# Expert stage of a Fourier filter and mixture of experts: low parts of the splits moved from GpSimd to VectorE, and both weight matrices laid out on the host in the order of the products

## The chip, the core and the metric

The kernel runs on one core of a Trainium2 chip. The metric is the device time in microseconds (us) of one execution; the median of three runs is given, and one more execution was profiled. The engines are named as in the profile: PE is TensorE (PEld its weight loads), DVE is VectorE, ACT is ScalarE, POOL is GpSimd, SP is SyncE. All inputs lie in device memory when the time starts, so what the host does to lay out an input is no part of the metric.

## The reference

Cut to what matters. First a filter along the sequence in the frequency domain, then a capacity-limited top-1 assignment of tokens to experts, then two products with a ReLU between them.

```python
x: (8, 2496, 256); filt_r, filt_i: (1249, 256); w_gate: (256, 8); w1: (8, 256, 1024); w2: (8, 1024, 256)
X = np.fft.rfft(x, axis=1)
y = np.fft.irfft(X * (filt_r + 1j * filt_i)[None], n=2496, axis=1)
x = y.reshape(19968, 256)
logits = x @ w_gate
# all (token, expert) pairs in falling order of logit; a token goes to the first expert
# that still has room, and each expert takes cap = 19968 // 8 = 2496 tokens
for e in range(8):
    mask = assigned == e
    h = np.maximum(x[mask] @ w1[e], 0.0)
    out[mask] = h @ w2[e]
```

## The kernel before

The first part, up to some 448 us of the profiled execution, is the filter: transforms as products on PE, the filter on DVE and POOL, the inverse transforms, and the filtered tokens written to a DRAM array `xs`. Nothing of it is touched by the change. `x` and the filter are already laid out on the host for it (`lay_x`, `lay_filter`).

The second part, the expert stage, handles the eight experts one after the other. An expert's 2496 tokens are taken in five groups of up to 512 (`g` = 0 to 4; the last has 448). For a group, POOL gathers the tokens' rows by indirect DMA into `xg` (line 784). PE transposes them (`ptr`, line 798, in `turn`). Then comes the first product, `pz` (line 820, eight blocks `f` of 128 hidden units), and the second, `py` (line 869). ACT copies `py` to `y`, and POOL writes `y` to the tokens' places by indirect DMA (line 880).

Every product is made in a reduced float32 form of three terms, high by high, high by low, and low by high. So each operand is split: a rounded copy, the high part, by ACT, and the difference from it, the low part, by another engine.

- Tokens: `xo` is the high part (ACT, line 801), `z` the low part (DVE, line 802).
- Hidden units: `hl` holds both. ACT writes the high half (line 826). The low half is written by DVE straight from PSUM (line 834; line 837 for the last group). For some blocks (odd `f` below 7, groups 1 to 3, while the routing of the next expert is in its search) ACT makes a second, unrounded copy `hr` (line 829) and POOL subtracts (line 830), since POOL can't read PSUM. There are 29 of these.
- Weights: `w0h`, `w0l` are the parts of the first matrix, `w1h`, `w1l` those of the second. An indirect DMA brings each matrix into `wr` (line 763, 128 partitions of 8 KB). `split` then handles eight pieces of 128x512 for an expert: high part on ACT (line 777), low part on POOL, except the first four pieces of the first expert, which are on DVE (line 778). A partition of `wr` holds two rows of `w1` as they lie in DRAM, and hidden units are taken eight apart. So the pieces of the first matrix are read with a step of eight elements and written densely. The columns of `xg` are taken two apart to match (line 796).

While PE works on one expert, the routing of the next runs beside it, most of it on DVE, with small products on PE (`rt`) in between. Its search has eleven rounds per expert (`counts`, `threshold`): `Gm` on DVE, a product, `t`, `D`, `X` on DVE, a product, then `mx`, `o`, `di`, `thr` on DVE. Then the assignment is updated (`M`, `tmp`, `ar`, `asg`, `val`, `r`, ...), and `places` makes the indices of the tokens in five steps: `oa` and `OH` on DVE, a product, `loc` on DVE, two sums on ACT (`junka`), `ex`, `js`, `xid`, `t1b`, `oid` on DVE. The eight weight pieces of the next expert are split in the same stretch of time.

PE's order in this stage is written out by hand: generators yield after a piece of work, and `Pump.feed` puts the next step of the routing between two pieces when a hand-set lag has passed. The order on ACT, DVE and POOL is made by the framework's scheduler. Each engine works through its own queue in order. `tc.issue_after` holds an instruction back to a point of the program.

Of the kernel before, what the change touches and what calls it, by code (L numbers as in the profile page):

```python
# [7 lines left out]
F32, F32R = mybir.dt.float32, mybir.dt.float32r  # L8
# [4 lines left out]
B, N, D, E8, FF = 8, 2496, 256, 8, 1024  # L13
# [96 lines left out]
def lay_filter(re, im):  # L110

    k, j = np.arange(K1)[:, None], np.arange(J)[None]
    fr = np.where(j < 32, k + 39 * j, 39 * (j - 31) - k)
    f = np.stack([np.asarray(re)[fr], np.asarray(im)[fr]])
    return np.ascontiguousarray(f.reshape(2, K1, J, 2, 128).transpose(4, 3, 1, 0, 2)).reshape(128, -1)


class Fft:
# [626 lines left out]
class Ffn:  # L745


    def __init__(s, tc, i, xs, out, cp, ww, zp, ps):
        s.tc, s.nc, s.xs, s.out, s.ww, s.zp, s.ps = tc, tc.nc, xs, out, ww, zp, ps
        s.w1 = i['moe_w1'].rearrange("e (q k) f -> (e q) (k f)", k=2)  # L750
        s.w2 = i['moe_w2'].rearrange("e (q f) d -> (e q) (f d)", f=8)
        s.id = cp.tile([128, 128], F32, name="id")
        make_identity(s.nc, s.id)
        s.scat = []
        s.wt, s.xg, s.xT = {}, {}, {}
# [9 lines left out]
    def split(s, e, part):  # L765

        nc = s.nc
        raw, hl = s.wt[e]
        k, h = divmod(part, 4)
        src, (hi, lo) = raw[k], hl[k]  # L770
        if k == 0:
            h, j = divmod(h, 2)
            src = src.rearrange("p (j q f) -> p j f q", j=2, f=8)[:, j, 4*h:4*h+4]
            hi, lo = (t.rearrange("p (j f q) -> p j f q", j=2, f=8)[:, j, 4*h:4*h+4] for t in (hi, lo))
        else:
            src, hi, lo = (t[:, 512*h:512*h+512] for t in (src, hi, lo))
        nc.scalar.copy(hi, src)
        (nc.gpsimd if e or part >= 4 else nc.vector).tensor_tensor(lo, src, hi.bitcast(F32), op=OP.subtract)

    def gather(s, e, g, ids):  # L780
        for t in range(4*g, 4*g + 4):
# [5 lines left out]
    def turn(s, e, g, h):  # L787

        nc = s.nc
        if h == 0:  # L790
            s.xT[e, g] = [s.zp.tile([128, 2, 512], F32R, name=t, tag=t, bufs=n) for t, n in (('xo', 2), ('z', 3))]
        p = s.ps.tile([128, 2, 256], F32, name="ptr", tag="c", bufs=4)
        w = 0
        for t in range(2):
            n = min(128, CAP - 128*(4*g+2*h+t))
            x = s.xg[e, 4*g+2*h+t].rearrange("p (q k) -> p k q", k=2)
            for k in range(2):
                nc.tensor.transpose(p[:, k, 128*t:128*t+n], x[:n, k], s.id[:n, :n])  # L798
            w += n
        hi, lo = (t[:, :, 256*h:256*h+w] for t in s.xT[e, g])  # L800
        nc.scalar.copy(hi, p[:, :, :w])
        return nc.vector.tensor_tensor(lo, p[:, :, :w], hi.bitcast(F32), op=OP.subtract).ins  # L802

    def run(s, e, pump, hook):
# [7 lines left out]
        def first(g, f):  # L812
            n = min(512, CAP - 512*g)
            xh, xl = s.xT[e, g]
            p = s.ps.tile([128, 512], F32, name="pz", tag="c", bufs=4)
            m = 0
            for k in range(2):
                sl = slice(1024*k+128*f, 1024*k+128*f+128)
                for w, x in ((w1h, xh), (w1h, xl), (w1l, xh)):
                    nc.tensor.matmul(p[:, :n], w[:, sl], x[:, k, :n], start=m == 0, stop=m == 5)  # L820
                    m += 1
                yield 0.65 * n / 512
            hl = s.wp.tile([128, 1024], F32R, name="hl", bufs=NH)
            hs.setdefault(g, []).append(hl)
            h, l = (hl[:, 512*k:512*k+512] for k in range(2))
            s.lasta = nc.scalar.activation(h[:, :n], p[:, :n], AF.Relu).ins  # L826
            if f % 2 == 1 and f < 7 and 0 < g < 4 and s.busy():
                r = s.wp.tile([128, 512], F32, name="hr", bufs=2)
                nc.scalar.activation(r[:, :n], p[:, :n], AF.Relu)
                nc.gpsimd.tensor_tensor(l[:, :n], r[:, :n], h[:, :n].bitcast(F32), op=OP.subtract)  # L830
            else:

                if g < 4:
                    nc.vector.scalar_tensor_tensor(l[:, :n], p[:, :n], 0.0, h[:, :n].bitcast(F32), op0=OP.max, op1=OP.subtract)  # L834
                else:
                    for a, b, c in ((384, n, n), (0, 384, 512)):
                        nc.vector.scalar_tensor_tensor(hl[:, c:c+b-a], p[:, a:b], 0.0, h[:, a:b].bitcast(F32), op0=OP.max, op1=OP.subtract)  # L837

        def firsts(g, count):
            for f in range(len(hs.get(g, ())), min(8, len(hs.get(g, ())) + count)):  # L840
# [50 lines left out]
def emit(tc, i, out):  # L891
    nc = tc.nc
    with ExitStack() as st:
# [31 lines left out]
        def after():  # L925
            nonlocal W
            q = 5
            for k in range(len(rest)):
                if k == 3 + NZ + MZ:
                    fst.close()  # L930
                    R.wb = pool(st, "rb", reuse_waits="tile")
                    W = Ffn(tc, i, xs, out, R.cp, pool(st, "ffw", reuse_waits="tile"), f.zp, ps)
                    W.busy = lambda: pump.kind in 'GX' and not split
                    f.zo = pool(zst, "zo", reuse_waits="tile")
                for c in f.inv2_parts(*rest[k], f.cps):
                    if q < 10:
# [140 lines left out]
                s.step_main()  # L1077


_INS = ['moe_w_gate', 'moe_w1', 'moe_w2']  # L1080


# [13 lines left out]
```

## Time and profile before

| | us |
|---|---|
| median of 3 runs | 1513.62 (1508.94 to 1519.25) |
| the profiled execution | 1514.13 |
| its span in the trace | 1512.4 |
| PE, PEld, DVE, ACT, POOL busy in it | 1411.4, 1234.2, 938.3, 714.0, 628.0 |

The span runs from the first instruction to the last, and 1.7 us of the profiled execution lie around it. A busy engine is one with an instruction under way; matmuls overlap, so PE can be busy and yet not at its peak. "Idle before" a group is the time in which its engine had nothing under way just ahead of it, and what is named behind the arrow ended that wait.

### The profile page before, as it was taken

How to read it: one execution, taken by the hardware profiler on the slowest of the kernel's cores; microseconds unless marked ns; L12 is line 12 of the kernel's file. 1: busy time of each engine (PE TensorE's matmuls, PEld its weight loads, DVE VectorE, ACT ScalarE, POOL GpSimd, SP SyncE). 2: the span in 40 equal slices, each digit the busy share in tenths (PEclk: the TensorE clock that was granted, in tenths of full speed). 3: DMA queues.
4: the chain of work that ended last, by engine and by line, in shares of the span. 5: the costliest groups of instructions: out<-in, count | busy, mean ns of one | idle time of the engine just before them, and what ended most of it. 6: DMA issues, size and time to landing. Idle time of an engine off the chain costs nothing.

```text
span 1512.4 us, 27201 instructions
## 1 busy us (share of the span) xinstructions
PE 1411.4 (93%) x10310; PEld 1234.2 (82%) x10310; DVE 938.3 (62%) x2500; ACT 714.0 (47%) x1705; POOL 628.0 (42%) x619
## 2 busy tenths in 40 slices
PE   4999999988977998999999899899899899999998
PEld 4998999965536887888798888798788789889998
DVE  3666676744567778667857977966866853532321
ACT  3666667634565345436424534533542544532332
POOL 0343344421006426544644654634635544433312
PEclk9999999998997999999999999899999999999999
DMA  9655663578992102102212112111211321111100
GB/s 267 187 150 132 168 179 71 138 214 252 339 349 88 44 31 86 58 20 91 62 34 77 46 52 82 46 44 38 91 32 52 115 72 48 38 49 41 44 25 27
DMA packets 56249, 150.61 MB, mean 100 GB/s; under 512 B 10824, under 2 KB 31432, under 8 KB 51921
## 3 DMA queue, kind: packets, MB, share of 16 engines
q0 software_dynamic: 17840, 60.34, 12.3%
q10 hardware_dynamic: 29407, 46.10, 10.1%
q1 hardware_dynamic: 8872, 42.44, 9.9%
q8 instruction: 81, 1.33, 0.4%
q14 instruction: 49, 0.40, 0.1%
HBM read 85.17 MB, written 63.70 MB: 98 GB/s over the span
## 4 chain that ended last, share of the span: by engine, by line
PE 64%; DVE 15%; ACT 7%; issue 7%; DMA 4%; ACTq 2%; POOL 1%; POOLq 0%; DVEq 0%; SPq 0%
PE py L869 22%; PE pz L820 21%; PE p L191 4%; PE pv L365 4%; PE p L204 3%; PE pa L259 2%; ACT Y L197 2%; PE ptr L798 2%; PE rt L528 2%; ACTq L273 2%; PE pa L223 2%; DVE hl L834 1%; ACT lg L688 1%; DMA xs<-xo 1%; DVE OH L719 1%
## 5 line engine op out<-in xcount | busy, mean ns | idle before, releaser
L869 PE MATMUL py<-w1h,hl 128*128 128x256 f32 x2496 | 490.0, 289 | 7.2 <-DVE hl L837 6.0
L869 PEld LDWEIGHTS py<-w1h,hl 128*128 128x128 f32 x2496 | 406.5, 193 | 11.1 <-DVE hl L837 7.4
L869 PE MATMUL py<-w1l,hl 128*128 128x256 f32 (+1 forms) x1280 | 361.8, 285 | 0.0
L880 POOL DMA_INDIRECT out<-y,oid x160 | 174.6, 1091 | 378.1 <-ACT y L879 335.8
L826 ACT ACTIVATE hl<-pz 128x512 fp32r<-128x512 f32 (+1 forms) x320 | 187.0, 587 | 227.9 <-PE pz L820 206.0
L820 PE MATMUL pz<-xo,w0h 128*128 128x512 f32 (+1 forms) x640 | 267.3, 418 | 15.2 <-DVE hl L834 5.5
L820 PE MATMUL pz<-z,w0h 128*128 128x512 f32 (+1 forms) x640 | 250.3, 391 | 0.8 <-DVE z L802 0.8
L820 PE MATMUL pz<-xo,w0l 128*128 128x512 f32 (+1 forms) x640 | 250.7, 392 | 0.0
L869 PEld LDWEIGHTS py<-w1l,hl 128*128 128x128 f32 (+1 forms) x1280 | 244.1, 191 | 1.9
L834 DVE SCALAR_TENSOR_TENSOR hl<-pz,hl 128x512 fp32r<-128x512 f32 x227 | 155.2, 687 | 130.1 <-ACT hl L826 129.5
L784 POOL DMA_INDIRECT xg<-xs,xid x160 | 168.7, 1055 | 98.1 <-PE ptr L798 33.6
L879 ACT COPY y<-py 128x256 f32<-128x256 f32 x152 | 56.2, 371 | 284.6 <-PE py L869 255.0
L820 PEld LDWEIGHTS pz<-xo,w0h 128*128 128x128 f32 x640 | 123.7, 193 | 36.1 <-DVE hl L834 7.7
L197 ACT COPY Y<-p 64x240 f32<-64x240 f32 (+1 forms) x304 | 116.0, 382 | 60.2 <-PE p L191 15.2
L820 PEld LDWEIGHTS pz<-xo,w0l 128*128 128x128 f32 x640 | 122.1, 191 | 24.5
L820 PEld LDWEIGHTS pz<-z,w0h 128*128 128x128 f32 x640 | 123.2, 192 | 17.0 <-DVE z L802 1.6
L191 PE MATMUL p<-cS,xr 117*128 117x120 f32 x688 | 102.9, 298 | 27.9 <-ACT Y L197 18.7
L212 POOL TENSOR_TENSOR P<-P 128x256 f32<-128x256 f32 x80 | 58.5, 731 | 167.5 <-DVE P L210 166.4
L191 PEld LDWEIGHTS p<-cS,xr 117*128 117x128 f32 x688 | 93.7, 212 | 32.2 <-ACT Y L197 21.6
L520 DVE TENSOR_TENSOR Gm<-M,thr 117x1232 bf16<-117x1232 f32 (+2 forms) x80 | 105.9, 1334 | 0.2
L729 ACT ACTIVATE junka<-rt,loc 128x176 bf16<-128x176 f32 x160 | 65.5, 410 | 70.5 <-DVE loc L726 43.9
L204 PE MATMUL p<-cW,Y 128*128 128x128 f32 x640 | 89.1, 278 | 0.6 <-ACT Y L197 0.6
(219 smaller groups left out, 2254.5 us busy)
## 6 DMA issues: line engine op xcount, KB each, us to landing
zd<-zt ACTq DMA_DIRECT2D x160, 128.0 KB
z<-zd SPq DMA_DIRECT2D x26, 600.0 KB
xs<-xo ACTq DMA_DIRECT2D x22, 600.0 KB
xr<-x SPq DMA_DIRECT2D x7, 1344.0 KB
xr<-x SPq DMA_DIRECT2D x7, 1064.0 KB
xs<-Y ACTq DMA_DIRECT2D x10, 600.0 KB
F<-filt ACTq DMA_DIRECT2D x2, 1280.0 KB
xg<-xs,xid POOLq DMA_INDIRECT x160, 2.8
```

The costliest lines, as they stand in the source:

```text
L191: s.lastmm = nc.tensor.matmul(p[:, q-q0, :120], xv[:, q-24*h], s.cS1, start=True, stop=True).ins
L197: (nc.vector.tensor_copy if t in ((5,) if b else (1, 3, 5, 7, 9)) else nc.scalar.copy)(dst, src)
L204: nc.tensor.matmul(p[:, k], s.Y1[b][:, 4*g+k, dh*128:dh*128+128], s.cW[:, 4*g+k], start=True, stop=True)
L365: nc.tensor.matmul(p[:120, :w], s.cD, z[:, g-g0:g-g0+w], start=True, stop=True)
L520: nc.vector.tensor_tensor(Gm[:, s0:s1, :m], s.M[:, s0:s1].unsqueeze(2).to_broadcast([117, s1 - s0, m]), thr[:117].unsqueeze(1).to_broadcas ...
L729: nc.scalar.activation(s.junka, pr[:, h, :S], AF.Sign, bias=loc[:, c:c+1], scale=-1.0, accum_out=js[:, c:c+1])
L784: s.lastg = s.nc.gpsimd.indirect_dma_start(out=xg[:n], out_offset=None, in_=s.xs, in_offset=bass.IndirectOffsetOnAxis(ap=ids[0][:n, t:t+1] ...
L820: nc.tensor.matmul(p[:, :n], w[:, sl], x[:, k, :n], start=m == 0, stop=m == 5)
L826: s.lasta = nc.scalar.activation(h[:, :n], p[:, :n], AF.Relu).ins
L834: nc.vector.scalar_tensor_tensor(l[:, :n], p[:, :n], 0.0, h[:, :n].bitcast(F32), op0=OP.max, op1=OP.subtract)
L869: nc.tensor.matmul(p[:a.stop-a.start], hs[g][f][:, a], b[:, 256*f:256*f+256], start=m == 0, stop=m == 8 * len(terms) - 1, skip_group_check ...
L880: st = nc.gpsimd.indirect_dma_start(out=out_rows, out_offset=bass.IndirectOffsetOnAxis(ap=ids[1][:w, 4*g+t:4*g+t+1], axis=0), in_=y[:w], i ...
```

## The change

Four edits, all for the expert stage.

1. The host lays out both weight matrices (`lay_w1`, `lay_w2`), so that partition q of `wr` holds rows q and 128+q of `w1`, and rows q, 128+q, ... of `w2`. The 8 KB of a partition are one run in DRAM, as before.
2. `split` reads and writes every piece densely. The pieces come in the same order as before.
3. The low part of every weight piece, and of every `hl`, is made on DVE. The second ACT copy `hr` goes.
4. `turn` takes the columns of `xg` as two halves instead of every other one.

```diff
+def lay_w1(w):
+    return np.ascontiguousarray(np.asarray(w).reshape(E8, 2, 128, FF).transpose(0, 2, 1, 3)).reshape(E8 * 128, 2 * FF)
+def lay_w2(w):
+    return np.ascontiguousarray(np.asarray(w).reshape(E8, 8, 128, D).transpose(0, 2, 1, 3)).reshape(E8 * 128, 8 * D)
...
-        s.w1 = i['moe_w1'].rearrange("e (q k) f -> (e q) (k f)", k=2)
-        s.w2 = i['moe_w2'].rearrange("e (q f) d -> (e q) (f d)", f=8)
+        s.w1, s.w2 = i['w1'], i['w2']
...
-        src, (hi, lo) = raw[k], hl[k]
-        if k == 0:
-            h, j = divmod(h, 2)
-            src = src.rearrange("p (j q f) -> p j f q", j=2, f=8)[:, j, 4*h:4*h+4]
-            hi, lo = (t.rearrange("p (j f q) -> p j f q", j=2, f=8)[:, j, 4*h:4*h+4] for t in (hi, lo))
-        else:
-            src, hi, lo = (t[:, 512*h:512*h+512] for t in (src, hi, lo))
+        o = 512 * (h if k else 2 * (h % 2) + h // 2)
+        src, hi, lo = (t[:, o:o+512] for t in (raw[k], *hl[k]))
         nc.scalar.copy(hi, src)
-        (nc.gpsimd if e or part >= 4 else nc.vector).tensor_tensor(lo, src, hi.bitcast(F32), op=OP.subtract)
+        nc.vector.tensor_tensor(lo, src, hi.bitcast(F32), op=OP.subtract)
...
-            x = s.xg[e, 4*g+2*h+t].rearrange("p (q k) -> p k q", k=2)
+            x = s.xg[e, 4*g+2*h+t].rearrange("p (k q) -> p k q", k=2)
...
-            if f % 2 == 1 and f < 7 and 0 < g < 4 and s.busy():
-                r = s.wp.tile([128, 512], F32, name="hr", bufs=2)
-                nc.scalar.activation(r[:, :n], p[:, :n], AF.Relu)
-                nc.gpsimd.tensor_tensor(l[:, :n], r[:, :n], h[:, :n].bitcast(F32), op=OP.subtract)
+            if g < 4:
+                nc.vector.scalar_tensor_tensor(l[:, :n], p[:, :n], 0.0, h[:, :n].bitcast(F32), op0=OP.max, op1=OP.subtract)
             else:
...
-                    W.busy = lambda: pump.kind in 'GX' and not split
```

The order of PE's and SP's instructions stays the same, row for row. Those of POOL, ACT and DVE move.

On POOL, a place in the handover from the first expert to the second, before (`wr` is the loaded weights, `xg` a gather, `out` a write of results):

```order
L784 DMA xg<-xs,xid 128x256 x4
L880 DMA out<-y,oid 19968x256
L778 TENSOR_TENSOR w0l<-wr_6668,w0h 128x512
L778 TENSOR_TENSOR w1l<-wr_6669,w1h 128x512 x2
L784 DMA xg<-xs,xid 128x256 x4
L880 DMA out<-y,oid 19968x256
L778 TENSOR_TENSOR w1l<-wr_6669,w1h 128x512
L880 DMA out<-y,oid 19968x256
```

and the same place now:

```order
L788 DMA xg<-xs,xid 128x256 x4
L878 DMA out<-y,oid 19968x256 x2
L788 DMA xg<-xs,xid 128x256 x4
L878 DMA out<-y,oid 19968x256 x2
L788 DMA xg<-xs,xid 128x256 x4
```

The subtractions between gathers and writes are gone; only indirect DMAs are left on POOL from here to the end.

On DVE, the same handover, before (`hl` 64 and 384 wide is the last group's low part, for which `py` waits; `OH` belongs to the places):

```order
L837 SCALAR_TENSOR_TENSOR hl<-pz,hl 128x64
L837 SCALAR_TENSOR_TENSOR hl<-pz,hl 128x384
L726 TENSOR_TENSOR loc<-sidx,rt 128x2
L730 TENSOR_SCALAR ex<-rt 128x4
L719 SCALAR_TENSOR_TENSOR OH<-iota,BC,oa 117x512
L837 SCALAR_TENSOR_TENSOR hl<-pz,hl 128x64
L837 SCALAR_TENSOR_TENSOR hl<-pz,hl 128x384
L694 TENSOR_TENSOR asg<-asg,u_6796 117x176
```

and now:

```order
L835 SCALAR_TENSOR_TENSOR hl<-pz,hl 128x64
L835 SCALAR_TENSOR_TENSOR hl<-pz,hl 128x384
L736 TENSOR_TENSOR loc<-sidx,rt 128x2
L729 SCALAR_TENSOR_TENSOR OH<-iota,BC,oa 117x512
L835 SCALAR_TENSOR_TENSOR hl<-pz,hl 128x64
L835 SCALAR_TENSOR_TENSOR hl<-pz,hl 128x384
L782 TENSOR_TENSOR w1l<-wr_6655,w1h 128x512
L740 TENSOR_SCALAR ex<-rt 128x4
```

A weight piece now stands between the `hl` pairs, and `ex` has moved behind it. The other seven pieces of this expert are spread over the same handover in the same way.

On DVE in the search for the second expert, before:

```order
L537 TENSOR_REDUCE D_5875<-t_5874 112x7
L538 TENSOR_TENSOR X_0_3654<-D_5875,row 112x49
L565 TENSOR_REDUCE mx_5807<-rt 128x7
L578 SCALAR_TENSOR_TENSOR o_5894<-mx_5807,pw 128x7
L580 TENSOR_REDUCE di<-o_5894 128x1
```

and now:

```order
L547 TENSOR_REDUCE D_5871<-t_5870 112x7
L548 TENSOR_TENSOR X_0_3654<-D_5871,row 112x49
L832 SCALAR_TENSOR_TENSOR hl<-pz,hl 128x512
L575 TENSOR_REDUCE mx_5805<-rt 128x7
L588 SCALAR_TENSOR_TENSOR o_5888<-mx_5805,pw 128x7
L590 TENSOR_REDUCE di<-o_5888 128x1
```

A low part that POOL made before now stands between `X` and `mx`, where DVE has handed a product to PE and needs its result next.

## Rows read from the trace of the kernel before

**Rows 1.** Page, busy time of PE over the span

```profile
PE 1411.4 (93%) x10310; PEld 1234.2 (82%) x10310; DVE 938.3 (62%) x2500; ACT 714.0 (47%) x1705; POOL 628.0 (42%) x619
```

**Rows 2.** Windows: stretch, length, busy PE, PEld, DVE, ACT, POOL, then PEclk, DMA

```profile
528.00:548.00 20.00, 20.00 (x160) 17.59 (x158) 14.65 (x37) 6.17 (x12) 4.52 (x4) 1.00 0.06 21
...
588.00:608.00 20.00, 15.84 (x111) 14.38 (x110) 15.27 (x48) 6.96 (x24) 12.02 (x11) 0.83 0.13 41
...
708.00:728.00 20.00, 17.55 (x115) 15.76 (x114) 20.00 (x53) 12.81 (x35) 17.61 (x14) 1.00 0.19 58
...
948.00:968.00 20.00, 16.68 (x103) 14.35 (x102) 18.92 (x44) 10.61 (x29) 16.97 (x12) 0.90 0.17 54
...
1208.00:1228.00 20.00, 19.20 (x118) 16.71 (x119) 12.52 (x46) 9.15 (x28) 11.25 (x11) 0.87 0.36 118
```

**Rows 3.** Waits of PE from 448 to 1512: total us, times, longest

```profile
PE rt L725 <- DVE ex L730: 7.7, 5, 4.6
...
PE py L869 <- DVE hl L837: 6.0, 5, 2.3
...
PE rt L528 <- DVE ex L730: 0.3, 1, 0.3
```

**Rows 4.** Timeline: DVE, POOL and PE around 588, PE at two other stalls

```profile
585.30 5.08 DVE L719 SCALAR_TENSOR_TENSOR OH<-iota,BC,oa 117x512 f16<-117x512 f16 x1
...
585.71 1.66 POOL L778 TENSOR_TENSOR w0l<-wr,w0h 128x512 fp32r<-128x512 f32 x1
587.33 2.50 POOL L778 TENSOR_TENSOR w1l<-wr,w1h 128x512 fp32r<-128x512 f32 x2
...
591.04 0.50 PE L869 MATMUL py<-w1h,hl 128*128 128x256 f32 x2 [2.33 <-DVE hl L837]
...
498.23 0.57 PE L528 MATMUL rt<-A,Gm 117*128 117x112 bf16 x8 [1.41 <-DVE Gm L520]
...
1291.86 0.38 PE L869 MATMUL py<-w1h,hl 128*128 128x256 f32 x1 [1.11 <-DVE hl L834]
```

**Rows 5.** One line of DVE: ns min/median/max, then its group with the mean

```profile
L733 DVE TENSOR_SCALAR js<-js x40: 151/160/3199, 442.2 to 1317.1; 128x4 f32<-128x4 f32 x40
...
L733 DVE TENSOR_SCALAR js<-js 128x4 f32<-128x4 f32 x40 | 18.3, 458 | 0.0
```

**Rows 6.** Lines: ns min/median/max, first and last start; the last row a group

```profile
L777 ACT CAST w0h<-wr x32: 1109/1204/1298, 456.8 to 1287.0; 128x512 fp32r<-128x512 f32 x32
L777 ACT CAST w1h<-wr x32: 610/622/648, 463.7 to 1289.7; 128x512 fp32r<-128x512 f32 x32
...
L778 DVE TENSOR_TENSOR w0l<-wr,w0h x4: 1077/1082/1092, 458.0 to 461.1; 128x512 fp32r<-128x512 f32 x4
...
L648 DVE TENSOR_TENSOR asg<-asg,ga x7: 328/334/336, 428.7 to 1173.3; 117x176 f32<-117x176 f32 x7
...
L609 DVE TENSOR_TENSOR tmp<-tmp,val x6: 1608/1612/3399, 468.9 to 1088.5; 117x1408 f32<-117x1408 f32 x6
...
L834 DVE SCALAR_TENSOR_TENSOR hl<-pz,hl 128x512 fp32r<-128x512 f32 x227 | 155.2, 687 | 130.1 <-ACT hl L826 129.5
```

**Rows 7.** Waits in the whole span: total us, times, longest

```profile
DVE t L536 <- PE rt L528: 70.8, 54, 2.6
...
DVE mx L565 <- PE rt L541: 46.3, 53, 2.6
...
POOL w0l L778 <- ACT w0h L777: 31.6, 10, 7.7
```

**Rows 8.** Timeline of the first expert's start: ACT, DVE, POOL, PE

```profile
456.82 4.21 ACT L777 CAST w0h<-wr 128x512 fp32r<-128x512 f32 x4 [8.93 <-DMA wr<-moe_w,widx]
...
457.99 4.16 DVE L778 TENSOR_TENSOR w0l<-wr,w0h 128x512 fp32r<-128x512 f32 x4 [10.75 <-ACT w0h L777]
...
458.87 0.98 POOL L784 DMA_INDIRECT xg<-xs,xid  x1 [0.30 <-issue]
...
462.05 0.80 PE L820 MATMUL pz<-xo,w0h 128*128 128x512 f32 x1 [2.14 <-ACT xo L801]
```

More of the change, by code (lines that the diff above doesn't have):

```diff
@@ L826, in first @@
             s.lasta = nc.scalar.activation(h[:, :n], p[:, :n], AF.Relu).ins
-            if f % 2 == 1 and f < 7 and 0 < g < 4 and s.busy():
-                r = s.wp.tile([128, 512], F32, name="hr", bufs=2)
-                nc.scalar.activation(r[:, :n], p[:, :n], AF.Relu)
-                nc.gpsimd.tensor_tensor(l[:, :n], r[:, :n], h[:, :n].bitcast(F32), op=OP.subtract)
-            else:
[L833 to L837, printed above, removed]
+            if g < 4:
+                nc.vector.scalar_tensor_tensor(l[:, :n], p[:, :n], 0.0, h[:, :n].bitcast(F32), op0=OP.max, op1=OP.subtract)
+            else:
+                for a, b, c in ((384, n, n), (0, 384, 512)):
+                    nc.vector.scalar_tensor_tensor(hl[:, c:c+b-a], p[:, a:b], 0.0, h[:, a:b].bitcast(F32), op0=OP.max, op1=OP.subtract)
         def firsts(g, count):
@@ L1077, in until @@
                 s.step_main()
-_INS = ['moe_w_gate', 'moe_w1', 'moe_w2']
+_INS = ['moe_w_gate']
 def kernel(**inputs):
@@ L1088 @@
     arrays.update(x=lay_x(inputs['x']), filt=lay_filter(inputs['filt_r'], inputs['filt_i']))
+    arrays.update(w1=lay_w1(inputs['moe_w1']), w2=lay_w2(inputs['moe_w2']))
     arrays.update(constants())
```

## The prediction

> **What bounds the kernel now.** I read the page's busy shares first: PE is busy 93% of the span [rows 1]. PE's order does not change, so the time can only move by PE's waits and by its clock. Next came the windows of 20 us. In a search stretch (528 to 548) PE is busy all 20.00 us with DVE at 14.65. Where one expert hands over to the next, PE loses time and DVE is nearly full: PE has 15.84 in 588 to 608, 17.55 in 708 to 728 with DVE at 20.00, 16.68 in 948 to 968 with DVE at 18.92 [rows 2]. From 1228 on, with almost no routing left, PE is nearly always full.
>
> The waits of PE say who is late. Between 448 and 1512 thirteen groups of waits end on DVE, the largest 7.7 us and the smallest 0.3, 40 us in all [rows 3]. The rest is 11 us for the first gather and 2 us for ACT. None of them ends on POOL.
>
> But POOL makes DVE late. The timeline at 585 shows it: `OH` starts on DVE at 585.30 and takes 5.08 us. POOL subtracts three weight pieces from 585.71 to 589.83, and `OH` ends half a microsecond later; then `hl` comes, then PE, which had waited 2.33 us [rows 4]. `js`, on four numbers a partition, has a median of 160 ns, a maximum of 3199 and a mean of 458: (458 - 160) x 40 = 11.9 us on one line [rows 5]. I summed the time above the usual for every DVE instruction from 440 us on. Of those more than 0.15 us over it, 57 overlap a POOL subtraction (`OH` at 585 is the longest), and they lose 72 us: some 60 next to weight pieces, 11 next to `hl`, the rest next to both a subtraction and an indirect DMA. Instructions of DVE that read PSUM, such as `hl`, are not among them. So DVE pays for the work that POOL was given to spare it.
>
> **The change, part by part.**
>
> Weight pieces on DVE: 60 move there (64 less the four that were there). No row shows a dense 128x512 subtraction of two SBUF operands. Two rows on either side bound it: `asg` with 176 columns at 334 ns and `tmp` with 1408 at 1612 [rows 6] lie on a line of 1.04 ns a column, which gives 0.68 us at 512. The stepped pieces on DVE, 1.08 us [rows 6], are the upper end. I take 0.68, since the step is gone. New work: 60 x 0.68 = 40.8 us; the four old ones fall by 4 x 0.40 = 1.6.
>
> Low parts of `hl` on DVE: 29 x 0.687 = 19.9 us [rows 6], all in the search.
>
> Taken from DVE: the 72 us. So DVE has 40.8 - 1.6 + 19.9 - 72 = -13 us net. It matters where: in the handovers +39 against -60, in the search +20 against -12.
>
> Handovers. For each stall of PE I followed DVE's unbroken run of work back from what ended it, summed the lost time in the run, and counted in the new order what now stands in the same run. At 585 to 595 PE stalls 1.68 + 2.33 + 0.31 + 1.52 = 5.84 us (the 2.33 in [rows 4]); the run holds 6.87 us of lost time and gets three pieces, 3 x 0.68 = 2.04. Net -4.8, so most of the stall goes. Nine such places, from 498 (1.41 us) to 1292 (1.11 us) [rows 4], hold 27.5 us of stalls, 36.0 of lost time and 15.0 of new work. Taking at each place the smaller of its stall and its net gain, 18 us go. The new order also moves routing work behind the awaited instruction (`tmp` at 966, the `js` group at 1209), worth some 5 us, and small stalls next to POOL give one more: -24 us. The ends are -15 (the net gain 36 - 15 = 21, less a quarter for new waits) and -31 (all of PE's stalls that stand next to POOL's arithmetic). Stalls with no lost time in front, at 695, 938 and 1182, 5.2 us together, stay.
>
> The clock. PE's granted clock falls to 1.2 GHz for some microseconds after a stall: 0.83 in 588 to 608, 0.90 in 948 to 968, 0.87 in 1208 to 1228 [rows 2]. Seven windows of this kind between them lose 20 x (1 - clock), together 17 us, of which PE was idle part of the time; some 15 us are real. The stalls at 938 and 1182 had no such fall, so not every stall costs it. If three quarters of the stalls go I take -9, with the ends -3 and -15.
>
> Start. ACT's four high parts of `w0` take 4.21 us in the first expert [rows 8]; dense they take the 622 ns of `w1h` instead of 1204 [rows 6], so 2.5. The token copies `xo` behind them, and so the first `pz` at 462.05 [rows 8], come forward by 1.7 at most; the second pair of transposes limits it to 1.5. Behind that the four `w1` pieces, 2.7 us, now stand on DVE ahead of `tmp`, where POOL's delays of 2.9 us fall away: nothing. Sum -1.5 (0 to -2.5).
>
> Here a rule speaks against the change. Next to four stepped subtractions of two SBUF operands on DVE, POOL issues indirect DMAs with gaps of 0.30 us [rows 8], and the four take 1077 to 1092 ns each [rows 6]: none waited for a DMA. The Trainium skill (SBUF — State Buffer, "SBUF: two separate sides") has a DVE instruction with two SBUF inputs and a GpSimd instruction that reads SBUF lock each other out of a shared port for the whole instruction. By that rule POOL's subtractions explain the 72 us, but the indirect DMAs, which read their indices from SBUF, would go on to hold up the new pieces; the sum would lose some 10 us of the gain on DVE (a rival, below). The trace agrees with the first half and not with the second.
>
> Search. The 19.9 us of `hl` go where DVE waits for PE: 70.8 us for `t` and 46.3 us for `mx` [rows 7]. The new order puts them there, ahead of `mx`, or behind `di`. Cover: these 117 us; without it each costs up to 0.69, 20 us in all. The other end is the 12 us of lost time in the same rounds. PE is full there now, so little can be won; I take +3 (+10 to -3).
>
> Nothing: ACT's 29 copies `hr` and its shorter `w0h` (ACT is busy 47% [rows 1]); POOL's gathers and writes, which come earlier but are not waited for after the first; the transposes, whose groups of four follow each other no slower than the dense ones of the filter; the weight loads, 128 runs of 8 KB as before.
>
> Sum, against the profiled execution: 1514.1 - 24 - 9 - 1.5 + 3 = 1482.6; that execution stands 0.5 above the median. **Forecast 1483 us.**
>
> **The rivals.**
>
> Everything goes: all stalls next to POOL and all falls of the clock, and the search costs nothing: 1514.1 - 31 - 15 - 2.5 = 1465. For it: lost time exceeds new work at nearly every stall. Against: pieces still stand in the chains on which PE waits, and a stall of 1 us suffices for some.
>
> A swap: DVE's queue is as full as before and only what fills it changes. If stalls shrink in proportion to DVE's net relief, 13 of 72, then 31 us give 5.6, and with the start 1.5: 1507. For it: DVE at 20.00 of 20 in 708 to 728, and six pieces in that run. Against: the count in the runs.
>
> DVE waits for ACT, and the kernel is slower. POOL now spends 31.6 us waiting for ACT's high parts of `w0` [rows 7]. On POOL nobody minds; on DVE a piece at the head of the queue holds up `hl`, for which PE waits. If DVE took all of it in the handovers: 41 + 32 against 60 lost, 13 us more on DVE than before, straight on PE where it stalls already, and some 6 more for clock: 1514 + 19 = 1533. It decides from the point where these waits exceed 60 - 39 = 21 us. Against it: in the new order most pieces stand behind instructions that, in the old trace, ran after ACT was done; by that comparison the others wait some 13 us, and ACT is faster now.
>
> The lock also holds against indirect DMAs. POOL is busy 42% of the span [rows 1], a third without the arithmetic that goes; 60 pieces, a third of them meeting an indirect DMA of some 0.98 us [rows 8] half done, make 10 us on DVE, half of it on PE: 1488, and 1490 with the clock. The rule is that of the Trainium skill cited above; [rows 6, 8] speak against it.
>
> That the change doesn't do what it says: PE's order is the same, all 89 subtractions stand on DVE and none on POOL, so I give it nothing.
>
> **How the numbers follow.** Forecast 0.57 (own range 1468 to 1499), everything goes 0.15, lock 0.03, swap 0.18, slower 0.07. The range leaves out the slower case, the lower half of "everything goes" and the ends of the swap: 1463 to 1508. A difference of 1% (15 us) is about what a measurement of this kernel can tell from none; the three runs spread over 0.7%. Faster by over 1%, below 1498.5: the forecast almost whole, everything, lock: 0.74. Within 1%: the swap and the forecast's upper end: 0.19. Slower: 0.07.
>
> **What the profile after would show.** `OH`, `js`, `tmp`, `t` on DVE with maxima near their medians; if the maxima stay, the step from POOL to DVE is wrong. Dense pieces at 0.68 us on DVE and 0.62 on ACT. DVE's busy time some 13 us lower. PE's waits on DVE at 15 us or so, and at least four of the seven falls of the clock gone. PE still full in the search; if `rt` there waits for `X` or `Gm`, the `hl` pieces cost more than I took. Waits of DVE's `w0l` and `w1l` for ACT over 20 us would mean the slower rival. The forecast is wrong if PE's stalls come from the length of the chain DVE, PE, ACT in `places` itself and not from DVE's lost time.

## The result and the profile after

The kernel after takes 1462.64 us (median of four runs, 1457.65 to 1466.76) where the kernel before took 1515.01 beside it: a ratio of 0.9657 with a 95% interval of 0.9628 to 0.9685. That is 52 us faster. The forecast was 1483, with a range from 1463 to 1508; the median lies 0.4 us under its low end.

The profiled execution of after took 1464.14 us with a span of 1461.9, 50.5 us less than the span before. The page's busy times and its row of PE's clock come first; they answer to [rows 1].

```profile
PE 1387.9 (95%) x10310; PEld 1214.2 (83%) x10310; DVE 912.8 (62%) x2589; ACT 682.9 (47%) x1676; POOL 493.2 (34%) x530
...
PEclk9999999998997999999999999999999999999999
```

PE does the same 10310 instructions in 23.5 us less busy time; some 16 us of that is time that it no longer spends at 1.2 GHz (table below). DVE has 89 instructions more and 25.5 us less busy time. The clock row has no digit below 9 after the thirteenth slice, where the experts begin. The row of before has one 8 there:

```profile
PEclk9999999998997999999999999899999999999999
```

The windows of 20 us, with the columns of [rows 2]. The work comes 4 us earlier than before in the first of them and 40 to 47 in the last, so one window does not hold the same instructions in both traces.

```profile
528.00:548.00 20.00, 20.00 (x158) 18.19 (x157) 15.25 (x38) 4.73 (x10) 2.96 (x3) 1.00 0.06 21
588.00:608.00 20.00, 19.46 (x135) 15.84 (x134) 17.42 (x63) 12.22 (x37) 15.65 (x15) 1.00 0.31 92
708.00:728.00 20.00, 19.01 (x152) 16.91 (x151) 15.78 (x62) 10.64 (x36) 12.58 (x12) 1.00 0.25 80
948.00:968.00 20.00, 19.03 (x155) 17.38 (x154) 14.19 (x71) 8.57 (x26) 6.59 (x6) 1.00 0.13 42
1208.00:1228.00 20.00, 20.00 (x138) 19.03 (x137) 6.61 (x17) 6.94 (x14) 7.59 (x8) 1.00 0.13 43
```

588 to 608 is the clearest: PE is busy 19.46 us of 20 instead of 15.84, at a clock of 1.00 instead of 0.83.

What PE waited for from 440 us on (answers to [rows 3]; total us, times, longest):

```profile
PE ptr L802 <- DMA xg<-xs,xid: 11.1, 1, 11.1
PE pz L824 <- DVE hl L832: 4.8, 3, 1.9
PE rt L538 <- DVE t1b L749: 2.3, 1, 2.3
...
PE rt L735 <- DVE ex L740: 0.9, 1, 0.9
```

The first gather still costs its 11 us. The waits on DVE add up to some 14 us where they were 40, and the largest of them in [rows 3], on `ex`, has gone from 7.7 to 0.9.

The DVE instructions that POOL used to stretch, and the weight pieces (ns min/median/max; answers to [rows 4 to 6]; the lines of the routing stand ten further down than before, those of the experts' block four, and two further up behind ACT's high part of `hl`):

```profile
L729 DVE SCALAR_TENSOR_TENSOR OH<-iota,BC,oa x40: 729/744/753, 434.5 to 1250.5; 117x512 f16<-117x512 f16 x40
...
L743 DVE TENSOR_SCALAR js<-js x40: 147/158/315, 442.8 to 1267.4; 128x4 f32<-128x4 f32 x40
...
L619 DVE TENSOR_TENSOR tmp<-tmp,val x6: 1608/1610/1618, 467.5 to 1052.5; 117x1408 f32<-117x1408 f32 x6
...
L781 ACT CAST w0h<-wr x32: 610/616/626, 457.7 to 1238.8; 128x512 fp32r<-128x512 f32 x32
...
L782 DVE TENSOR_TENSOR w0l<-wr,w0h x32: 673/683/693, 458.3 to 1239.6; 128x512 fp32r<-128x512 f32 x32
L782 DVE TENSOR_TENSOR w1l<-wr,w1h x32: 669/680/724, 465.7 to 1242.1; 128x512 fp32r<-128x512 f32 x32
```

Every maximum now stands within 0.16 us of its median: `OH` at 753 ns (5.08 us at 585 before), `js` at 315 (3199 before), `tmp` at 1618 (3399). The dense piece costs 0.68 us on DVE and 0.62 on ACT, as forecast.

**Where the time went.** I cut the stretch from the first `pz` to the end into three: the gaps on PE; half of the time in which PE was busy at 1.2 GHz, which is about what the lower clock took (in before, products of `pz` follow each other by 227 ns at 2.4 GHz and by 426 at 1.2, medians); and the rest, in which some 5 us behind PE's last product are counted. All are summed from the trace's records of PE and of the granted clock, one profiled execution of each kernel.

| us | first `pz` at | first `pz` to end | PE's gaps | lost to the clock | rest |
|---|---|---|---|---|---|
| before | 462.0 | 1050.3 | 40.9 | 18.3 | 991.1 |
| after | 460.9 | 1001.0 | 14.1 | 2.4 | 984.5 |
| difference | -1.1 | -49.3 | -26.8 | -15.9 | -6.6 |

Instruction by instruction of PE, the two traces keep step within 2 us between the handovers; the gain comes in six jumps of 3.5 to 8 us, one at each handover from 590 to 1210 of before, with some 4 us ahead of them and 3 behind.

### The profile page after: what moved, and what is told of

It reads as the page before. It is cut to its first block, busy times and chain, and to the rows that moved or that the text cites. A ratio compares the mean times of both kernels' runs of the same rounds, so it can differ in the third digit from the quotient of the medians.

```text
span 1461.9 us, 27147 instructions
## 1 busy us (share of the span) xinstructions
PE 1387.9 (95%) x10310; PEld 1214.2 (83%) x10310; DVE 912.8 (62%) x2589; ACT 682.9 (47%) x1676; POOL 493.2 (34%) x530
## 4 chain that ended last, share of the span: by engine, by line
PE 68%; DVE 9%; issue 9%; ACT 6%; DMA 4%; ACTq 2%; POOL 2%; POOLq 0%; SPq 0%; DVEq 0%
PE py L867 23%; PE pz L824 22%; PE p L201 4%; PE pv L375 4%; PE p L214 4%; PE pa L269 2%; ACT Y L207 2%; PE rt L538 2%; PE ptr L802 2%; ACTq L283 2%; PE pa L233 2%; POOL out L878 1%; DMA xs<-xo 1%; ACT lg L698 1%; DMA wr<-w,widx 1%
## 5 line engine op out<-in xcount | busy, mean ns | idle before, releaser
L867 PE MATMUL py<-w1h,hl 128*128 128x256 f32 x2496 | 482.6, 286 | 1.1 <-DVE hl L835 1.0
L867 PEld LDWEIGHTS py<-w1h,hl 128*128 128x128 f32 x2496 | 401.1, 191 | 3.9 <-DVE hl L835 1.7
L878 POOL DMA_INDIRECT out<-y,oid x160 | 171.9, 1074 | 495.6 <-ACT y L877 461.2
L824 PE MATMUL pz<-xo,w0h 128*128 128x512 f32 (+1 forms) x640 | 263.9, 412 | 6.5 <-DVE hl L832 4.8
L832 DVE SCALAR_TENSOR_TENSOR hl<-pz,hl 128x512 fp32r<-128x512 f32 x256 | 174.9, 687 | 127.4 <-ACT hl L830 126.5
L867 PEld LDWEIGHTS py<-w1l,hl 128*128 128x128 f32 (+1 forms) x1280 | 241.1, 188 | 1.9
L788 POOL DMA_INDIRECT xg<-xs,xid x160 | 176.4, 1102 | 127.0 <-issue 44.5
L222 POOL TENSOR_TENSOR P<-P 128x256 f32<-128x256 f32 x80 | 58.5, 732 | 172.4 <-DVE P L220 171.3
L214 PEld LDWEIGHTS p<-cW,Y 128*128 128x128 f32 x640 | 80.2, 193 | 2.3 <-issue 1.0
```

The source lines that it names most:

```text
L214: nc.tensor.matmul(p[:, k], s.Y1[b][:, 4*g+k, dh*128:dh*128+128], s.cW[:, 4*g+k], start=True, stop=True)
L222: nc.gpsimd.tensor_tensor(P[:, :, :64], P[:, :, :64], P[:, :, 64:], op=OP.subtract)
L788: s.lastg = s.nc.gpsimd.indirect_dma_start(out=xg[:n], out_offset=None, in_=s.xs, in_offset=bass.IndirectOffsetOnAxis(ap=ids[0][:n, t:t+1] ...
L867: nc.tensor.matmul(p[:a.stop-a.start], hs[g][f][:, a], b[:, 256*f:256*f+256], start=m == 0, stop=m == 8 * len(terms) - 1, skip_group_check ...
L878: st = nc.gpsimd.indirect_dma_start(out=out_rows, out_offset=bass.IndirectOffsetOnAxis(ap=ids[1][:w, 4*g+t:4*g+t+1], axis=0), in_=y[:w], i ...
```

## The experiments

None of the kernels leaves any work out. On a first occasion (e1 to e4) the kernel before took 1514 us, as in the result. On a second, of three series (e5 to e8, e9 to e11, e12), it took 1528, 1529 and 1532. The record numbers the chips: e1 to e4 and e12 have the same number, the others another, so the number does not tell the occasions apart. e9 is the kernel after itself on the second occasion, 1492.95 us, and e5 to e11 are compared with it and not with 1462.64. Between kernels I compare the time from the first `pz` to the end of the profiled executions, since the stage ahead of it varies by some us from run to run. Each of these is one execution, and the executions of one kernel differ by 4 to 12 us, so a difference of a few us between two of them is weak by itself.

### e1 to e4: the change in its parts

e1, the weight pieces back on POOL, the rest as after:

```diff
-        nc.vector.tensor_tensor(lo, src, hi.bitcast(F32), op=OP.subtract)
+        (nc.gpsimd if e or part >= 4 else nc.vector).tensor_tensor(lo, src, hi.bitcast(F32), op=OP.subtract)
```

> The changed kernel, but the low parts of the weight pieces go back to POOL (dense, all but the first four); the hl parts stay on DVE. Theory A (POOL's subtractions hold up DVE): the dense pieces keep POOL at them for some 77 us against 95 before, so DVE's lost time comes back to some 45 to 50 us, PE's stalls to 20 us or more with falls of the clock: 1495 to 1510 us. Theory B (the gain comes from the dense layout, faster ACT copies and less stepping): 1475 us or less, and DVE's maxima stay near their medians.

e2, the 29 low parts of `hl` back on ACT and POOL, the rest as after:

```diff
-            if g < 4:
+            if f % 2 == 1 and f < 7 and 0 < g < 4 and s.busy():
+                r = s.wp.tile([128, 512], F32, name="hr", bufs=2)
+                nc.scalar.activation(r[:, :n], p[:, :n], AF.Relu)
+                nc.gpsimd.tensor_tensor(l[:, :n], r[:, :n], h[:, :n].bitcast(F32), op=OP.subtract)
+            elif g < 4:
...
+                    W.busy = lambda: pump.kind in 'GX' and not split
```

> The changed kernel, but the 29 hl parts go back to ACT's second copy and POOL's subtraction; the weight pieces stay on DVE. Theory A: some 11 us of lost time come back in the search, where DVE waits for PE anyway, so the time stays within 5 us of the changed kernel, 1460 to 1468 us. Theory C (the hl parts on DVE cost PE time in the search, as the prediction took with 3 us): 1455 to 1460 us.

e3 has both edits, so that only the new layouts are left of the change.

> The layouts and dense pieces alone: both kinds of subtraction stay on POOL as in the kernel before. Theory A: little of the gain, since POOL's subtractions still meet DVE's: 1495 to 1512 us. Theory B: most of the gain, 1475 us or less.

e4 has the old layouts of both weight matrices and so the stepped reading in `split`, with all arithmetic on DVE (against after):

```diff
-        s.w1, s.w2 = i['w1'], i['w2']
+        s.w1 = i['moe_w1'].rearrange("e (q k) f -> (e q) (k f)", k=2)
+        s.w2 = i['moe_w2'].rearrange("e (q f) d -> (e q) (f d)", f=8)
...
-            x = s.xg[e, 4*g+2*h+t].rearrange("p (k q) -> p k q", k=2)
+            x = s.xg[e, 4*g+2*h+t].rearrange("p (q k) -> p k q", k=2)
```

> The kernel before in its old layout, with every low part on DVE: no arithmetic on POOL, but the 32 pieces of the first matrix are read with a step of eight elements, by ACT at 1.2 us and by DVE at 1.08 us. Theory A: most of the gain, less some 13 us of longer pieces on DVE, a third of it on PE: 1464 to 1478 us. Theory B: 1490 us or more.

| | time | ratio to before (95%) | first `pz` to end | gaps | clock | rest |
|---|---|---|---|---|---|---|
| e1 | 1490.24 | 0.9827 (0.9788 to 0.9866) | 1028.2 | 31.3 | 11.0 | 985.9 |
| e2 | 1468.83 | 0.9700 (0.9652 to 0.9747) | 1008.0 | 17.5 | 5.3 | 985.2 |
| e3 | 1500.26 | 0.9903 (0.9868 to 0.9937) | 1035.4 | 33.3 | 16.1 | 986.0 |
| e4 | 1481.51 | 0.9767 (0.9729 to 0.9805) | 1018.9 | 20.9 | 8.6 | 989.4 |

e1 came out five microseconds under the range of its theory A and far from B, e2 0.8 above A's, e3 in A's, e4 three and a half above A's. In the stretch from the first `pz` the parts add up well. Taking the pieces off POOL gives 27.4 us with the 29 low parts on POOL (e3 to e2) and 27.2 without (e1 to after). Taking those low parts off gives 7.2 (e3 to e1) and 7.0 (e2 to after). The layouts give 14.9 with POOL's arithmetic (before to e3) and 17.9 without (e4 to after). The smallest part, the seven us, is clear in the times of e3 and e1 (1497.02 to 1500.73 against 1485.35 to 1491.23), and not in those of e2 and after, which overlap.

e1 and e3 show the pieces' mechanism alone: with dense pieces on POOL, 1.3 us each, `OH` is as stretched as before. The lines of `OH` in e1 and in e3:

```profile
L729 DVE SCALAR_TENSOR_TENSOR OH<-iota,BC,oa x40: 737/746/4748, 433.6 to 1276.8; 117x512 f16<-117x512 f16 x40
```

```profile
L729 DVE SCALAR_TENSOR_TENSOR OH<-iota,BC,oa x40: 735/745/4756, 433.3 to 1283.8; 117x512 f16<-117x512 f16 x40
```

In e1 DVE lost some 52 us next to pieces, against 61 before, and was spared 60 x 0.68 = 41 us of work. So moving the pieces to POOL cost DVE only some 11 us net, but PE 27. In e2 DVE loses 12 us next to POOL's subtractions; PE's gaps rise by 3.4 us and the clock's part by 2.9. `X` at 629 and 1020 us and `w` at 904 take 1.98, 1.42 and 1.31 us next to a POOL subtraction, where `X` has a median of some 0.2 elsewhere; PE waits 0.5 and 0.7 us for the two `X`. At 915 PE stalls 2.34 us ahead of a `pz`, where it stalls 1.44 in after, with the slow clock behind it; whether the late `w` or ACT's added copies led there, I did not separate. The other fall, at 833, stands at a stall of 2.27 us that after has too (2.25 at 836) without a fall. So the move of the low parts is worth some 7 us, but how it comes about is shown for the smaller part of it.

### e5: POOL subtracts for nobody

```diff
+        j = s.wp.tile([128, 512], F32, name="junk", bufs=2)
+        nc.gpsimd.tensor_tensor(j, src, hi.bitcast(F32), op=OP.subtract)
```

> The kernel after with work added: beside each of the 64 weight pieces GpSimd subtracts the same two tiles once more into a scratch tile that nobody reads, so nothing waits for GpSimd's result. Theory A (VectorE is held up while GpSimd subtracts, whoever uses the result): VectorE again loses 40 to 55 us next to these, PE's waits on it rise from 14 to 25 us or more, falls of the clock come back, and the time is 1485 to 1515. Theory B (the old kernel was late because GpSimd delivered the low parts late, in a chain with ScalarE): the time stays at 1460 to 1468 and OH, js, tmp keep maxima near their medians.

1550.40 us, a ratio of 1.0132 (1.0096 to 1.0168) to before, 57 us above e9 and further than theory A had it. Nothing waits for the scratch tile, so lateness of POOL's results is not what hurts. The lines of the subtractions and of the pieces on DVE:

```profile
L784 POOL TENSOR_TENSOR junk<-wr,w0h x32: 1279/1298/2692, 463.3 to 1325.0; 128x512 f32<-128x512 f32 x32
...
L782 DVE TENSOR_TENSOR w1l<-wr,w1h x32: 670/680/4916, 467.7 to 1332.3; 128x512 fp32r<-128x512 f32 x32
```

A piece that takes 0.68 us takes up to 4.92 beside them. 55 DVE instructions lose 71.5 us next to these subtractions; PE's gaps rise from 33.1 (e9) to 72.9 us and the clock's part from 9.9 to 26.5. From the first `pz` to the end that is 58.5 us, 0.82 us for each us that DVE lost. POOL's gathers and writes, which now queue behind these subtractions, are not the way: behind the first `pz`, PE's waits put 2.4 us to a gather and 0.9 to `y`, and some 67 to DVE.

### e6: POOL writes and reads nothing

```diff
+        j = s.wp.tile([128, 512], F32, name="junk", bufs=2)
+        for _ in range(2):
+            nc.gpsimd.memset(j, 0.0)
```

> The kernel after with work added: beside each of the 64 weight pieces GpSimd fills a scratch tile of 128x512 with zeros, twice; it reads nothing and nobody reads the tile. If any GpSimd arithmetic instruction on SBUF holds up VectorE, OH and tmp overlapping a fill are stretched by the fill's length as they were by subtractions, and the time is 1475 to 1500. If only GpSimd's reading of two tiles does, OH stays within 760 ns, tmp within 1620, and the time is 1460 to 1467.

1483.53 us, a ratio of 0.9706 (0.9678 to 0.9735), 9 us under e9. The fills wait for nothing, so they did not stay beside the pieces: POOL ran all 128 in trains between 449 and 556 us, and the time says little about handovers. From the first `pz` to the end it equals e9 (1029.5 and 1030.3); 4.9 us of the difference lie ahead of the experts, which the edit hardly touches. But one train shows what a fill does. The timeline around it, of POOL and of DVE:

```profile
469.72 9.87 POOL L785 MEMSET junk<- 128x512 f32 x21
...
471.50 0.74 DVE L729 SCALAR_TENSOR_TENSOR OH<-iota,BC,oa 117x512 f16<-117x512 f16 x1
...
475.63 0.15 DVE L740 TENSOR_SCALAR ex<-rt 128x4 f32<-128x4 f32 x1
475.70 3.92 DVE L743 TENSOR_SCALAR js<-js 128x4 f32<-128x4 f32 x1
```

`OH`, with SBUF operands only, takes its usual 0.74 us in the middle of the train. `ex`, which reads PSUM, is not touched either. `js`, one SBUF input and an SBUF output, stands for 3.92 us, to the end of the train; the only other of its kind that met one, `Gm` at 549, took 4.03. So it is not POOL's being busy that holds DVE up, but which two instructions meet. The Trainium skill (SBUF — State Buffer, "SBUF: two separate sides") says that a DVE instruction with two SBUF inputs and GpSimd exclude each other only where GpSimd's instruction reads SBUF, and one in a two-port mode wherever GpSimd has the shared port. The trace agrees for `OH` (0.74 us) and is in line with it for `js` (3.92 us), though no row names the mode.

### e7: each piece twice on DVE

```diff
+        j = s.wp.tile([128, 512], F32, name="junk", bufs=2)
+        nc.vector.tensor_tensor(j, src, hi.bitcast(F32), op=OP.subtract)
```

> The kernel after with work added: VectorE does each of the 64 weight pieces a second time into a scratch tile, 64 x 0.68 = 43 us more on VectorE, all in the handovers. Moving the pieces to GpSimd cost 28 us though VectorE lost only 51 - 41 = 10 us by it. Theory A (it is where the delay falls: GpSimd stretched the very instructions PE was waiting for, while the pieces stand where there is some slack): less than the 28 us, 1470 to 1488. Theory B (VectorE's total in the handover decides, and it is full there): about one us for each, 1495 to 1515.

1506.30 us, a ratio of 0.9863 (0.9829 to 0.9897), 13 us above e9; from the first `pz` 16.7. That is theory A's size (7 to 25 us above the kernel after) and not B's. 64 x 0.68 = 43.5 us of added DVE work cost 16.7, 0.38 us for each, less than half of the price of a delayed us in e5; some 11 us net by way of POOL cost 27 in e1. As I read it, work that stands in the order at the pieces' place has some slack, and the delays by POOL hit `OH`, `js`, `X`, on which PE's next product waits.

### e8 to e12: the layouts one by one, and the controls

e8, the first matrix in its natural order, so that the transposes read every second column (e10 is the same kernel again):

```diff
-    return np.ascontiguousarray(np.asarray(w).reshape(E8, 2, 128, FF).transpose(0, 2, 1, 3)).reshape(E8 * 128, 2 * FF)
+    return np.ascontiguousarray(np.asarray(w).reshape(E8, 128, 2, FF)).reshape(E8 * 128, 2 * FF)
...
-            x = s.xg[e, 4*g+2*h+t].rearrange("p (k q) -> p k q", k=2)
+            x = s.xg[e, 4*g+2*h+t].rearrange("p (q k) -> p k q", k=2)
```

> The kernel after, with the first weight matrix handed over in its natural order again (rows 2q and 2q+1 on partition q), so that the transposes of the tokens read every second column; the second matrix, the dense pieces and VectorE's work stay as after. Theory A (the 4 to 5 us by which PE's time outside waits and slow clock is shorter in the dense layouts come from the transposes): groups of four transposes go from 0.354 back to 0.386 us, PE's time outside waits and slow clock rises by 2.5 to 5 us from 984.5, and the time is 1464.5 to 1468. Theory B (it is something else in the layout): groups stay at 0.354, time 1461 to 1464.

e9, the kernel after unchanged:

> The kernel after unchanged, as a control beside the next two, since e8 lost 17 us against its own control where its slower transposes account for 3. Theory A (the ratio of 0.966 holds wherever the two kernels are compared): 0.963 to 0.969 of the time before, some 14 us of waits of PE behind the first gather, one or two falls of the clock. Theory B (e8's extra waits were those of its chip and moment): 0.970 or more, and stalls of PE that no instruction ends between 490 and 510 us, as e8 shows them.

> The same kernel as e8, beside the control e9. Theory A (the natural order of the first weight matrix costs some 17 us by itself, of which 3 are slower transposes and the rest new waits in the handovers): 12 to 20 us above e9, with waits of PE of 20 us or more behind the first gather and three falls of the clock. Theory B (only the transposes cost, and the rest of e8 was its chip and moment): 2 to 6 us above e9, waits of PE and falls of the clock as in e9.

e11, the second matrix in its natural order, so that the pieces of `w0` are read in steps:

```diff
-    return np.ascontiguousarray(np.asarray(w).reshape(E8, 8, 128, D).transpose(0, 2, 1, 3)).reshape(E8 * 128, 8 * D)
+    return np.ascontiguousarray(np.asarray(w).reshape(E8, 128, 8, D)).reshape(E8 * 128, 8 * D)
...
-        o = 512 * (h if k else 2 * (h % 2) + h // 2)
+            src = src.rearrange("p (j q f) -> p j f q", j=2, f=8)[:, j, 4*h:4*h+4]
```

> The kernel after with the second weight matrix handed over in its natural order, so that the pieces of w0 are read at steps of 32 bytes again (1.08 us on VectorE and 1.2 on ScalarE where dense ones take 0.67 and 0.62); the transposes stay dense. Both layouts together cost 19 us (e4). Theory A (the pieces are what the layout is worth): 10 to 18 us above e9. Theory B (the transposes are): 0 to 6 us above e9. Where e8 and this one each come out at over 10 us, the two are not a sum, and the waits are what a small shift of any kind does to the handovers.

e12, the kernel before unchanged:

> The kernel before unchanged, with a profile of its own, to see why it gained 52 us by the change in the first series and 36 us in the series of e5 to e11, where the kernel after stood still between 491 and 499 us and at some places in the handovers where PE's results reached VectorE and ScalarE late. Theory A (that is of the series and meets both kernels; before loses more too, but hides part of it under waits that it has anyway): a time of 1522 to 1532, PE's gaps from the first product of the experts on at 45 to 60 us instead of 41, stalls that no instruction ends between 490 and 510 us here too. Theory B (the kernel before is not touched by it): gaps of some 41 us as in the first profile, the added time lying before the experts. If the time is near 1514, the run is of the first kind of series, and this stays open.

| | time | ratio to before (95%) | first `pz` to end | gaps | clock | rest |
|---|---|---|---|---|---|---|
| e8 | 1492.54 | 0.9769 (0.9744 to 0.9794) | 1027.1 | 26.8 | 9.2 | 991.1 |
| e9 (after) | 1492.95 | 0.9757 (0.9719 to 0.9794) | 1030.3 | 33.1 | 9.9 | 987.3 |
| e10 (as e8) | 1493.12 | 0.9761 (0.9726 to 0.9797) | 1031.0 | 27.1 | 13.0 | 990.8 |
| e11 | 1502.62 | 0.9821 (0.9774 to 0.9868) | 1038.4 | 37.2 | 12.3 | 988.8 |
| e12 (before) | 1531.01 | 0.9994 (0.9964 to 1.0025) | 1070.0 | 52.6 | 23.6 | 993.8 |

Read against 1462.64, e8 seemed to cost 30 us. The control e9 took that back: the kernel after is as slow there, theory B of e9, and e8 and e10 equal it in time. So both ranges of e8 were missed in time, and e10 lies below both of its ranges. The transposes do cost: the four of a group take 0.386 us in steps and 0.354 dense (medians of some 50 undisturbed groups between `pz` products), and the rest rises by 3.8 and 3.5 us. The line of the transposes in e9 and then in e10 (busy us, mean ns):

```profile
L802 PE MATMUL ptr<-id,xg 128*128 128x128 f32 (+1 forms) x320 | 49.6, 277 | 12.7 <-DMA xg<-xs,xid 11.3 <-DVE hl L832 1.4
```

```profile
L802 PE MATMUL ptr<-id,xg 128*128 128x128 f32 (+1 forms) x320 | 53.9, 289 | 12.3 <-DMA xg<-xs,xid 10.9 <-DVE hl L832 1.3
```

PE's gaps are 6 us shorter in both, so that nothing of it is left in the time; why, these two traces do not settle. e11 is 9.7 us above e9, just under theory A's range, and the intervals of the two ratios overlap. PE's gaps are 4.1 us longer, and the stepped pieces take 1.1 to 1.2 us; that these lengthen the chains in the handovers again is likely and not shown. If the two layouts add up, they are worth some 10 us on the second occasion and not the 19 of the first; e4 itself was not run there.

e9 and e12 give the whole change on the second occasion: 1070.0 - 1030.3 = 39.7 us from the first `pz` (36 by the medians of the times), of which gaps 19.5, clock 13.7 and rest 6.5. The occasion adds 29 us to after and 20 to before, theory A of e12. The first of it is in the first expert, where PE stands still inside groups of products and no instruction releases it. The timeline of PE in e9:

```profile
491.69 0.41 PE L538 MATMUL rt<-A,Gm 117*48 117x112 bf16 x5 [0.63 <-issue]
...
493.13 0.26 PE L538 MATMUL rt<-A,Gm 117*48 117x112 bf16 x2 [1.03 <-issue]
495.25 0.28 PE L867 MATMUL py<-w1l,hl 128*128 128x256 f32 x1 [1.53 <-issue]
```

The profile of before on that occasion has them too, and in its waits they are put down to the same:

```profile
PE py L869 <- issue: 2.7, 4, 1.1
```

## Why the prediction was right, and where its sizes were off

**From POOL to DVE: right.** The lost time of DVE, 72 us by the prediction's count, is gone with POOL's subtractions, comes back with them in e1 and e3, and comes with subtractions that nobody uses in e5. DVE's busy time fell by 25.5 us over the whole span, nearly twice the 13 of the sum; a part of the difference is that DVE's instructions overlap a little, so that four pieces in a row take 2.50 us at 458 and not 2.72. The forecast's other signs (maxima near the medians, 0.68 and 0.62 us a piece, PE's waits on DVE near 15 us, PE full in the search) are all in the profile.

**Handovers, -24 (-15 to -31): right.** PE's gaps fell by 26.8 us, 3.4 of which belong to the search by e2; on the second occasion by 19.5. What was said to stay stayed: the stalls at 695, 938 and 1182 of before stand at 682, 916 and 1142 of after with 1.40, 1.44 and 1.49 us (before 1.50, 2.32 and 1.41) and a little more beside the first.

**The clock, -9 (-3 to -15): this step was too small.** It measured -15.9, of which 15.1 are the seven falls of before and 0.8 the one at the start, and -13.7 on the second occasion. That the falls cost some 15 us was right; the prediction took three quarters of it and then less, on the thought that a stall of 1 us suffices for some. In the trace of after none of the seven is left. In part that is luck. Before, four of the seven stand at one stall each (1.72, 3.32, 4.61 and 4.63 us, at 828, 966, 1089 and 1209), while the stall of 2.32 at 938 has none; in after no stall behind the first gather is longer than 2.25 us. But the longest of after stands in e9, the same kernel, too, and there the clock falls to 1.2 GHz for 3.4 us. The stall in after and in e9, and the windows around them, with granted clocks of 1.00 and 0.91:

```profile
835.87 0.48 PE L538 MATMUL rt<-A,Gm 117*48 117x64 bf16 x11 [2.25 <-DVE t1b L749]
```

```profile
857.16 0.48 PE L538 MATMUL rt<-A,Gm 117*48 117x64 bf16 x11 [2.25 <-DVE t1b L749]
```

```profile
831.00:851.00 20.00, 17.57 (x151) 15.94 (x151) 14.80 (x67) 9.23 (x30) 8.31 (x7) 1.00 0.15 45
```

```profile
852.00:872.00 20.00, 17.75 (x135) 15.81 (x134) 14.86 (x66) 8.32 (x29) 6.97 (x7) 0.91 0.12 37
```

The same holds for the stalls of 1.40 and 0.37 us at 682 (after, no fall) and 699 (e9, a fall at 701). Each of these two falls costs 1.7 us. On the second occasion e9 has four falls behind the first `pz` and e12 nine.

**Search, +3 (+10 to -3): the wrong sign.** The 29 low parts were taken to cost a little on DVE, since PE was full there. e2, and e1 against e3, have their move at -7; these are no further us but stand in the gaps (3.4 by e2, 2.0 by e1 and e3) and in the clock (2.9 and 5.1) of the table. PE stays full in 528 to 548 with the low parts on DVE, as predicted. What was missed is that POOL's 29 subtractions took 12 us from DVE at `X`, `Gm`, `w` and others (e2). PE waits 1.6 us for `X` in e2 and not at all in after; the rest of the 7 us was not traced to single delays, and some of it is the luck of the clock.

**Transposes at nothing: wrong by 3.5 us.** The prediction compared the stepped groups of four with the filter's and saw no difference. Against the same groups dense there is one, 0.386 to 0.354 us; e8 and e10 put it at 3.5 to 3.8 us of the rest. Of the 6.6 us in the rest, e11 gives 1.5 more to the pieces' layout, and before against e4 (991.1 to 989.4) 1.7 to POOL's arithmetic; these last two are near what the sum can tell.

**Start, -1.5 (0 to -2.5): the mechanism right, the size not to be told.** The first `pz` came 1.1 us earlier (460.9 for 462.0 in [rows 8]), but e2, whose start is that of after, has it at 456.4, and e9 and e12 at 463.4 and 463.3. ACT's four high parts take 2.18 us there instead of 4.21, as the timeline of after has it:

```profile
457.65 2.18 ACT L781 CAST w0h<-wr 128x512 fp32r<-128x512 f32 x4 [9.19 <-DMA wr<-w,widx]
```

**The rivals.** "Everything goes", at 1465 and a chance of 0.15, is what the first occasion showed: all falls of the clock and most stalls. The forecast's errors at the clock, the search and the transposes all point the same way, which put the result at the very end of the range. On the second, where the two stand 36 us apart (1528.91 and 1492.95), the forecast's own case, 31 us, is the nearer. The swap's condition came true and its price did not. What stood in 708 to 728 of before comes 12.5 us earlier in after, and DVE is as full there:

```profile
695.50:715.50 20.00, 19.01 (x129) 17.50 (x128) 20.00 (x61) 11.92 (x36) 14.05 (x11) 1.00 0.20 63
```

DVE has 61 instructions in it for 53, and PE is busy 19.01 us for 17.55. So DVE's queue is full in this handover as before, and yet PE loses less: a delay by POOL struck whatever DVE had next, while the added pieces can stand behind what PE awaits. The swap's time, 1507, is 44 us off. DVE waiting for ACT came to less than the 21 us from which it decides; the wait of the whole span, most of it the start:

```profile
DVE w0l L782 <- ACT w0h L781: 14.2, 5, 10.5
```

The lock against indirect DMAs did not come: POOL spends 171.9 us in those of `out` and 176.4 in those of `xg`, and of 64 pieces on DVE the slowest took 0.72 us.

## What to carry to other kernels

Before giving an engine's work away, look at what its neighbour's instructions take while the helper runs: a mean far above the median (`js`, 458 ns for 160) is a price that no wait in the profile shows. Count such a price by where it falls: 71.5 us of delays cost 58.5 us of time, while 43.5 us of plain added work at the pieces' place cost 16.7. A full queue on the helped engine is by itself no sign that nothing was won. And run the control beside the experiment: the same two kernels differed by 3.4% on one occasion and 2.4% on another, and a kernel that read as 30 us slower took the time of the kernel after, to within a microsecond, once both ran on one occasion.

## What the runs showed of the hardware that was not expected

- GpSimd's fills left VectorE's instructions with two inputs alone (`OH` 0.74 us within a train of 21 fills) and held up `js`, with one input, for 3.92 us, through several fills and not only the one that it met.
- Next to GpSimd's subtractions a VectorE subtraction of 0.68 us took up to 4.92 us (e5): from 739.42 to 744.34, with three subtractions on GpSimd from 739.99 to 743.77. So it too waits through a whole train. It began 0.57 us ahead of the first, as `OH` at 585 did by 0.41 [rows 4], and both ended some 0.55 us behind the last; spans on GpSimd are rough, so which of the two came first is open.
- A transpose of tokens with every second column read is slower: 0.386 us for four against 0.354.
- On the second occasion PE stood still for 2.5 to 4.5 us in all between 488 and 505 us, within groups of products and with nothing that released it, in both kernels (e5, e7 to e12; e6 has no such stalls). No transfer of instructions runs between 490 and 500 us (e9, e10, e12). In the handovers of e9 ScalarE and VectorE took up PE's results 1 to 2 us late (`y` at 606.83 us after 2.65 us of idling, 0.42 in after). The cause was not found: no row of the profile names what ends these waits.
